# Layer 1's output factor taken from the gated rows' norms, and margins on TensorE's inputs in a list schedule

## The chip, the cores and the metric

One core of one Trainium2 chip runs the whole program. The metric is device time in microseconds (us) of one launch; lower is better. The engines are TensorE (PE, with its weight loads PEld), VectorE (DVE), ScalarE (ACT), GpSimd (POOL) and the queue of SyncE (SP), which issues every DMA.

## What is computed

A top-32 attention over 4 batches of 8 heads, 576 positions of width 64, and behind it two gated layers on the 2304 rows of width 512, each with an inner width of 1536:

```python
scores = q @ k.T / sqrt(64)
kth = np.partition(scores, -32, axis=-1)[..., -32:-31]
attn = softmax(where(scores >= kth, scores, -1e9))
x = (attn @ v) as (2304, 512)
xn = x / sqrt(mean(x * x) + 1e-6) * rms_g
g = xn @ w_gate
x = (g * sigmoid(g) * (xn @ w_val)) @ w_out
out = (sigmoid(x @ w_gate2) * (x @ w_val2)) @ w_out2
```

## The kernel before

Matrix operands are split into two float16 parts, a high and a low one; a product is the sum of three (high by high, high by low, low by high). A part pair needs a scale, a power of two got from a norm, so that its values lie well in float16.

**The work.** The rows come in 18 units of 128. Attention takes a unit in two halves of four tiles. A tile is a head by 128 rows: the score matmuls into `sp` (two buffers of PSUM), VectorE's rounds of maximum and replacement (`m8`, `w`), ScalarE's exponential `e`, the mask on VectorE, the split on ScalarE and POOL into `ph`, a DMA transpose into `pt`, and the product with V into `pv` (`attend`, L687). `enter1` (L801) normalizes a finished unit's rows, splits them into `sn` and has a DMA transpose them into `xt`. `gate1` (L884) does this and, for three pieces j of the inner width, calls `gated` (L839): a product into `pg` and one into `pw`, 48 matmuls each, the tanh and copies by ScalarE, products by POOL into `sg`, and the split into `ht`. `out1` (L892) multiplies the three pieces back into `py` with 144 matmuls and splits it into `yt`. `gate2` and `out2` do the same for layer 2, whose weights `wl` are read again from DRAM for each batch of two units; `out2` adds into `po`.

**The factor.** The scale for the split of `py` comes from `py` itself: ScalarE squares it with a sum per row (`ysq`; the squares go to a scrap tile `junk` under the tag `sn`, the buffer that also holds `enter1`'s input of the transpose), TensorE sums over the partitions with a matrix of ones (`yn`), VectorE makes a power of two of it, and only then ScalarE scales `py` into `sf`:

```python
nc.scalar.activation(junk, py, AF.Square, accum_out=ysq)
t = ps_m.tile([P, 1], F32, name="yn", tag="mm", lane="yn")
nc.tensor.matmul(t, lhsT=ones32, rhs=ysq, start=True, stop=True)
...
s, i = pow2_scale(m, 1, "y")
nc.scalar.activation(f, py, AF.Copy, scale=s)
```

**Buffers.** `pg`, `pw`, `py`, `po`, `yn`, the norms `kvt` and the products of the weight preparation share three banks of PSUM (tag `mm`). The float32 temporaries `wf`, `g`, `sv`, `sf` share four buffers of SBUF (tag `tmp`); `sg` has two, the output tile `acc` two, attention's `xr` one.

**The order.** Nothing is issued as it is written. `Scheduler.record` (L171) notes every operation with its inputs, a cost in ns and a priority that comes from its place in the program, and `order` (L234) plays them forward on a clock of its own: it always takes the operation that can start first, among those of one engine by priority. An operation can start when its inputs are there (L336), its engine is free and a buffer is free for the tile that it opens. Each engine then executes its list strictly in that order. The weights of both layers are converted and scaled in the first part (`prep1`, `prep2`, L541 and L554), beside the first units' attention.

Of the kernel before, what the change touches and what calls it, by code (L numbers as in the profile page):

```python
# [18 lines left out]
P = 128  # L19
# [26 lines left out]
OWN = 130.0  # L46

# [10 lines left out]
BATCHES = (1,) + (2,) * 8 + (1,)  # L58
# [77 lines left out]
class Scheduler:  # L136
# [97 lines left out]
    def order(self):  # L234
# [60 lines left out]
        while len(out) < len(self.ops):  # L295
# [39 lines left out]
            for u in op.users:  # L335
                u.start = max(u.start, op.end + OWN if u.eng == op.eng != "sync" else done)  # L336
# [20 lines left out]
def topk_attention_moe_kernel(  # L357
# [108 lines left out]
    def prep_piece(w, kind, j, g, s, i, place, held, ways):  # L466
# [305 lines left out]
    def attention_rest(b, kv, sc, x):  # L772
# [19 lines left out]
        xr = xp.tile([P, 4, D], F32, name="xr", bufs=1)  # L792
# [8 lines left out]
    def enter1(x):  # L801

        xf = x.rearrange("p h d -> p (h d)")
# [8 lines left out]
        f = m1.tile([P, 512], F32, name="sf", tag="tmp", bufs=4, lane="sfxt")  # L812
# [3 lines left out]
        t = mo.tile([P, 2 * NC, P], F16, name="xt", bufs=1)  # L816
        nc.sync.dma_start_transpose(out=t, in_=n.rearrange("p a d -> p (a d)"))
        return t

    def product(ps, w, xt, start=True, stop=True):  # L820

        with E.group():
            for m in range(4):
                n = 0
                for c in range(4):
                    for l, r in ((c, 0), (c, 1), (c + 4, 0)):
                        nc.tensor.matmul(
                            ps[:, m],
                            lhsT=w[c][:, 512 * r + P * m : 512 * r + P * m + P],
                            rhs=xt[:, l],  # L830
                            start=n == 0,
                            stop=n == 11,
                        )
                        n += 1

    def flat(t):
        return t.rearrange("p m r -> p (m r)")

    def gated(xt, wg, wv, gsc, vsc, silu, name, bufs, last=False, behind=None):  # L839
# [3 lines left out]
        pg = ps_m.tile([P, 4, P], F32, name="pg", tag="mm", lane=name)  # L843
        if behind is not None:
            E.after(behind)
        product(pg, wg, xt)
# [3 lines left out]
        ht = htp.tile([P, 2, CPJ, P], F16, name=name, bufs=bufs)  # L850
        hi, lo = (ht[:, a].rearrange("p m r -> p (m r)") for a in range(2))
        pw = lambda: ps_m.tile([P, 4, P], F32, name="pw", tag="mm", lane=name)
        if last:
            pw = pw()
            product(pw, wv, xt)
# [3 lines left out]
            return ht.rearrange("p a m r -> p (a m) r")  # L859
        if silu:  # L860
            g = m1.tile([P, 512], F32, name="g", tag="tmp", bufs=4, lane="g" + name)
            nc.scalar.activation(g, pg, AF.Copy, scale=gsc)
# [4 lines left out]
        product(pw, wv, xt)  # L867
        sv = m1.tile([P, 512], F32, name="sv", tag="tmp", bufs=4, lane="sv" + name)
# [5 lines left out]
        return ht.rearrange("p a m r -> p (a m) r")  # L874
# [9 lines left out]
    def gate1(u, j):  # L884
        if j == 0:
            in1[u] = enter1(xs[u])
        gsc, vsc, _ = state["c1"]
        ht1[u, j] = gated(
            in1[u], lay1["g"][0][j], lay1["v"][0][j], gsc[:, j : j + 1], vsc[:, j : j + 1], True, "ht1", 3, behind=vsc if u < 2 else None
        )  # L890

    def out1(u):  # L892

        ik = state["c1"][2]
        py = ps_m.tile([P, 4, P], F32, name="py", tag="mm", lane="y")
        with E.group():
            for m in range(4):
                n = 0
                for j in range(NJ):
                    for c in range(4):  # L900
                        for l, r in ((c, 0), (c, 1), (c + 4, 0)):
                            nc.tensor.matmul(
                                py[:, m],
                                lhsT=lay1["o"][0][j][c][:, 512 * r + P * m : 512 * r + P * m + P],
                                rhs=ht1[u, j][:, l],
                                start=n == 0,
                                stop=n == 12 * NJ - 1,
                            )
                            n += 1
        py = flat(py)  # L910
# [7 lines left out]
        s, i = pow2_scale(m, 1, "y")  # L918
        f = m1.tile([P, 512], F32, name="sf", tag="tmp", bufs=4, lane="sfyt")
        nc.scalar.activation(f, py, AF.Copy, scale=s)  # L920
        yt = mo.tile([P, 2, 512], F16, name="yt", bufs=2)
        nc.scalar.activation(yt[:, 0], f, AF.Copy)
        nc.gpsimd.tensor_tensor(out=yt[:, 1], in0=f, in1=yt[:, 0], op=ALU.subtract)
# [4 lines left out]
        in2[u] = (yt.rearrange("p a (c r) -> p (a c) r", r=P), gsc, a)  # L928
# [10 lines left out]
    def gate2(b, u, j):  # L939
        for n in "gv":  # L940
            if (b, n, j) not in w2:
                load2(b, n, j)
        yt, gsc, _ = in2[u]
        last = b == len(batches) - 1
        ht2[u, j] = gated(
            yt, w2[b, "g", j], w2[b, "v", j], gsc[:, j : j + 1], state["c2"][0][:, j : j + 1], False, "ht2", 6, last,
            state["c2"][0] if b == 0 else None
        )

    def out2(b, us):  # L950

        po = {}
        for j in range(NJ):
            load2(b, "o", j)
            for u in us:
                if j == 0:
                    po[u] = ps_m.tile([P, 512], F32, name="po", tag="mm", lane="o")
                w, n = w2[b, "o", j], 0
                with E.group():
                    for c in range(4):  # L960
                        for l, r in ((c, 0), (c, 1), (c + 4, 0)):
                            nc.tensor.matmul(
                                po[u],
                                lhsT=ht2[u, j][:, l],
                                rhs=w[c][:, 512 * r : 512 * r + 512],
                                start=j == 0 and n == 0,
                                stop=j == NJ - 1 and n == 11,
                            )
                            n += 1
        for u in us:  # L970
            osc = tmul(in2[u][2], state["c2"][1], name="osc")
            o = mo.tile([P, 512], F32, name="acc")
            nc.scalar.activation(o, po[u], AF.Copy, scale=osc)
            for dst, rows in dests[u]:
                nc.sync.dma_start(dst, o[rows])


    xs, dests, in1, in2, ht1, ht2, w2, acc, state = {}, {}, {}, {}, {}, {}, {}, {}, {}
    E.prio = -2 * TAU
    gr = m1.tile([P, 512], F32, name="gr", tag="tmp", bufs=4, lane="gr")  # L980
# [48 lines left out]
    batches = [[next(units) for _ in range(n)] for n in BATCHES]  # L1029
    first = lambda us: [(8.1 if j == NJ else 5.4, *((out1, (u,)) if j == NJ else (gate1, (u, j)))) for u in us for j in range(NJ + 1)]  # L1030
    second = lambda b, us: [(5.4, gate2, (b, u, j)) for j in range(NJ) for u in us] + [(7.8 * len(us), out2, (b, us))]
# [3 lines left out]
    for b in range(len(batches) + 1):  # L1035
        lists = [second(b - 1, batches[b - 1]) if b else [], first(batches[b]) if b < len(batches) else []]
# [37 lines left out]
```

## Time and profile before

| | |
|---|---|
| runs | 1255.1, 1255.52, 1259.76 us; median 1255.52 |
| profiled execution | span 1257.2 us, 41569 instructions; the page gives no time of this execution beside its span |
| TensorE busy, by 40 equal slices | `3776474599999999999999999998999999999998` |
| VectorE busy | `6999998897988989888988899787799888970001` |
| granted TensorE clock | `9788576799999999999999999998999999999999` |

The slices are 31.4 us wide and give the busy share in tenths, 9 for 90% or more; the clock is in tenths of full speed. Matmuls are pipelined and their ends are modelled, so the distance from start to start tells more than a duration. A wait is put down to whatever came last.

### The profile page before, as it was taken

To read this page: it belongs to the slowest core of one execution; us is meant where nothing else is said; L and a number is where in the kernel's file an instruction comes from. 1 tells how busy PE (TensorE), PEld (TensorE's weight loads), DVE (VectorE), ACT (ScalarE), POOL (GpSimd) and SP (SyncE) were. 2 spreads that over 40 slices of the span, in tenths; PEclk is the share of its full clock that TensorE was granted. 3 is DMA by queue.
4 is the path that set the end of the run, shared out by engine and by line. 5 is a ranking of instruction groups with operands and counts; after the bars stand their busy time and mean duration, and the time that the engine had idled before them with its cause. 6 is when DMAs were issued, how large, how long until landed. Compare 5 with 4: busy or idle time off the path is not lost.

```text
span 1257.2 us, 41569 instructions
## 1 busy us (share of the span) xinstructions
PE 1128.0 (90%) x17020; PEld 967.0 (77%) x17020; DVE 1006.8 (80%) x2553; ACT 835.8 (66%) x1464; POOL 844.2 (67%) x966
## 2 busy tenths in 40 slices
PE   3776474599999999999999999998999999999998
PEld 2443364598789879969986998798879969997976
DVE  6999998897988989888988899787799888970001
ACT  6999888776596747677854766575847655662531
POOL 6997899887586847685864668475847665761530
PEclk9788576799999999999999999998999999999999
DMA  8986898698977575688978486768685775754337
GB/s 266 289 300 178 232 253 234 177 280 205 203 179 148 131 179 128 146 187 185 225 123 193 110 150 136 180 130 175 139 178 128 152 181 111 183 124 134 136 110 269
DMA packets 323774, 225.26 MB, mean 179 GB/s; under 512 B 278400, under 2 KB 286592, under 8 KB 323584
## 3 DMA queue, kind: packets, MB, share of 16 engines
q1 hardware_dynamic: 323584, 222.62, 72.7%
q8 instruction: 133, 2.18, 0.7%
q14 instruction: 57, 0.47, 0.1%
HBM read 147.06 MB, written 14.16 MB: 128 GB/s over the span
## 4 chain that ended last, share of the span: by engine, by line
PE 45%; DVE 13%; ACT 11%; DMA 10%; POOL 10%; issue 7%; SPq 2%; POOLq 0%; ACTq 0%; DVEq 0%
PE pw L353 13%; PE pg L353 12%; PE po L353 7%; PE py L353 6%; DVE m L353 5%; DVE w L353 4%; DMA pt<-ph 4%; POOL ph L353 3%; POOL sg L353 3%; PE sp L353 3%; PE pv L353 3%; DMA xt<-sn 2%; SPq L353 2%; DMA qt<-qn 2%; POOL ht L353 2%
## 5 line engine op out<-in xcount | busy, mean ns | idle before, releaser
L353 DVE MAX8 m<-w 128x8 f32<-128x576 f32 x432 | 318.1, 751 | 4.3
L353 PEld LDWEIGHTS <-wl 128*128 128x128 f16 x5184 | 294.4, 98 | 3.5 <-issue 1.9
L353 POOL TENSOR_TENSOR ph<-e,ph 128x512 f16<-128x512 f32 (+1 forms) x288 | 204.8, 733 | 86.5 <-ACT ph L353 83.6
L353 DVE MATCH_REPLACE8 w<-m,w 128x576 f32<-128x576 f32 x288 | 213.5, 743 | 0.0
L353 POOL TENSOR_TENSOR sg<-sg,sv 128x512 f32<-128x512 f32 x105 | 133.7, 1274 | 50.2 <-ACT sv L353 47.0
L353 ACT ACTIVATE e<-sp,nb,sc 128x576 f32<-128x576 f32 x144 | 117.3, 829 | 73.1 <-POOL nb L353 37.7
L353 PEld LDWEIGHTS <-w1v 128*128 128x128 f16 (+1 forms) x2640 | 150.2, 98 | 12.3 <-issue 7.5
L353 PE MATMUL pg<-xt,w1g 128*128 128x128 f16 x2592 | 155.7, 221 | 2.9 <-ACT sv L353 1.9
L353 PE MATMUL pg<-yt,wl 128*128 128x128 f16 x2592 | 156.0, 221 | 1.7 <-ACT sv L353 0.8
L353 PE MATMUL pw<-xt,w1v 128*128 128x128 f16 x2592 | 153.5, 219 | 3.6 <-ACT sv L353 3.0
L353 PEld LDWEIGHTS <-w1g 128*128 128x128 f16 (+1 forms) x2624 | 151.4, 99 | 3.7 <-issue 2.3
L353 PE MATMUL pw<-yt,wl 128*128 128x128 f16 x2592 | 153.6, 219 | 0.6 <-ACT sg L353 0.3
L353 POOL TENSOR_TENSOR ht<-sg,ht 128x512 f16<-128x512 f32 x105 | 121.8, 1161 | 45.7 <-ACT ht L353 43.6
L353 PEld LDWEIGHTS <-w1o 128*128 128x128 f16 (+1 forms) x2640 | 150.2, 99 | 1.8 <-DVE w1g L353 1.4
L353 PE MATMUL py<-ht,w1o 128*128 128x128 f16 x2592 | 148.9, 220 | 0.0
L353 PE MATMUL po<-wl,ht 128*128 128x512 f16 x648 | 145.1, 379 | 0.0
L353 PE MATMUL sp<-kt,qt 128*128 128x512 f16 (+3 forms) x640 | 97.8, 300 | 44.7 <-DVE e L353 36.3
L353 ACT ACTIVATE ph<-e 128x576 f16<-128x576 f32 x144 | 97.2, 677 | 53.0 <-DVE e L353 47.1
L353 DVE MAX8 m<-sp 128x8 f32<-128x576 f32 x144 | 108.0, 758 | 28.8 <-PE sp L353 27.9
L353 DVE SCALAR_TENSOR_TENSOR e<-sp,m,e 128x576 f32<-128x576 f32 x144 | 115.6, 810 | 6.2 <-ACT e L353 2.9
L353 PEld LDWEIGHTS <-qt 128*128 128x128 f16 (+1 forms) x640 | 51.3, 104 | 88.8 <-DVE e L353 29.4
L353 PEld LDWEIGHTS <-ht 128*128 128x128 f16 x648 | 61.4, 98 | 69.0
(167 smaller groups left out, 1824.8 us busy)
## 6 DMA issues: line engine op xcount, KB each, us to landing
wl<-w2g SPq DMA_DIRECT2D x60, 512.0 KB, 5.1
wl<-w2v SPq DMA_DIRECT2D x60, 512.0 KB, 4.9
wl<-w2o SPq DMA_DIRECT2D x60, 512.0 KB, 5.0
raw<-in_moe_w_gate_dram SPq DMA_DIRECT2D x24, 512.0 KB, 5.0
raw<-in_moe_w_val_dram SPq DMA_DIRECT2D x24, 512.0 KB, 5.1
raw<-in_moe_w_out_dram SPq DMA_DIRECT2D x24, 512.0 KB, 4.8
qr<-in_q_dram SPq DMA_DIRECT2D x32, 128.0 KB, 2.9
kr<-in_k_dram SPq DMA_DIRECT2D x16, 256.0 KB, 4.5
```

The lines of the kernel that those rows point to most:

```text
L353: getattr(eng, method)(*map(real, a), **{n: real(x) for n, x in k.items()})
```

## The change

Three things change; the other new code (units in groups, halves of a group) is not used here, since every group in `BATCHES` is a single unit, for which the products and their order inside a group are those of before.

- `out1` takes the factor of its split from the gated rows. `gated` squares `sg` in place behind its split, with a sum per row into a column of `hsq` (54 Squares); `out1` adds the three columns on VectorE (`hn`), and `yn` sums that. The factor is the norm's with 2^32 for a bound of the weights, and is there whether `py` is or not. The Square of `py` and its scrap tile go.
- In `order`, past 250000 ns of the planner's own clock, an input of a matmul counts as there 1000 ns later if an engine made it, 2500 ns later if a DMA brought it. Only the order changes; no wait is added. Buffers that come free get no such margin.
- `tmp` has three buffers instead of four; `sg` has three instead of two, which `xr` and `acc` now share.

```diff
+SLACK = (1000.0, 2500.0, 250000.0)
...
             for u in op.users:
-                u.start = max(u.start, op.end + OWN if u.eng == op.eng != "sync" else done)
+                late = SLACK[op.eng == "sync"] if u.eng == "tensor" and op.end > SLACK[2] else 0.0
+                u.start = max(u.start, op.end + OWN if u.eng == op.eng != "sync" else done + late)
...
-                t = m1.tile([P, 512], F32, name="wf", tag="tmp", bufs=4, lane="wf")
+                t = m1.tile([P, 512], F32, name="wf", tag="tmp", bufs=3, lane="wf")
...
-        xr = xp.tile([P, 4, D], F32, name="xr", bufs=1)
+        xr = mo.tile([P, 512], F32, name="xr", tag="sg", bufs=3, lane="xr")[:, 0 : 4 * D].rearrange("p (h d) -> p h d", d=D)
...
-        sg = mo.tile([P, 512], F32, name="sg", lane=name)
+        sg = mo.tile([P, 512], F32, name="sg", bufs=3, lane=name)
...
         nc.scalar.activation(hi, sg, AF.Copy)
         nc.gpsimd.tensor_tensor(out=lo, in0=sg, in1=hi, op=ALU.subtract)
+        if sq is not None:
+            nc.scalar.activation(sg, sg, AF.Square, accum_out=sq)
...
-        ysq = tiny.tile([P, 1], F32, name="ysq")
-        junk = m1.tile([P, 1024], BF16, name="junk", tag="sn", lane="yt")[:, 0:512]
-        nc.scalar.activation(junk, py, AF.Square, accum_out=ysq)
-        t = ps_m.tile([P, 1], F32, name="yn", tag="mm", lane="yn")
-        nc.tensor.matmul(t, lhsT=ones32, rhs=ysq, start=True, stop=True)
-        m = tiny.tile([P, 1], F32, name="ym")
-        nc.vector.tensor_scalar(m, t, 2.0 ** -30, None, op0=ALU.max)
+            n = tiny.tile([P, 1], F32, name="hn")
+            nc.vector.tensor_reduce(n, hsq[b], axis=mybir.AxisListType.X, op=ALU.add)
+            t = ps_m.tile([P, 1], F32, name="yn", tag="mm", lane="yn")
+            nc.tensor.matmul(t, lhsT=ones32, rhs=n, start=True, stop=True)
+            m = tiny.tile([P, 1], F32, name="ym")
+            nc.vector.tensor_scalar(m, t, 2.0 ** -60, 2.0 ** 32, op0=ALU.max, op1=ALU.mult)
...
-            o = mo.tile([P, 512], F32, name="acc")
+                o = mo.tile([P, 512], F32, name="acc", tag="sg", bufs=3, lane="acc")
```

In the orders below a number behind a name is that of a buffer; `wl` is a weight of layer 2, `w1v` and `w1o` are weights of layer 1.

**First place.** TensorE, at the norm of the unit whose `yn` starts at 868.02 us in the trace of before. Before:

```order
L353 MATMUL sp_17721<-kt_17320,qt_17416 64x64
L353 MATMUL kvt_17738<-kvn_17714,ones_0_107 128x1
L353 MATMUL yn_17744<-ysq_17730,ones_0_107 128x1
L353 LDWEIGHTS wl_3164_16889
L353 MATMUL pg_17756<-yt_15208,wl_3164_16889 128x128
```

In the change:

```order
L355 LDWEIGHTS wl_3142_16877
L355 MATMUL pw_17412<-yt_16370,wl_3142_16877 128x128
L355 MATMUL yn_17482<-hn_17332,ones_0_107 128x1
L355 LDWEIGHTS w1o_19_211
L355 MATMUL py_17484<-ht_3109_16560,w1o_19_211 128x128
```

Before, `yn` came after `py` and some attention work; now it comes right ahead of the first matmul of `py`, and reads `hn`.

**Second place.** TensorE, at the last tile of a half of attention, whose `pv` starts at 636.76 us in the trace of before. Before, with the end of the tile ahead of it:

```order
L353 LDWEIGHTS pt_12430
L353 MATMUL pv_12229<-vt_10828,pt_12430 128x65
L353 MATMUL yn_12564<-ysq_12466,ones_0_107 128x1
L353 LDWEIGHTS pt_12477
L353 MATMUL pv_12229<-vt_10828,pt_12477 128x65
```

In the change:

```order
L355 LDWEIGHTS w1v_18_182
L355 MATMUL pw_12725<-xt_12438,w1v_18_182 128x128
L355 LDWEIGHTS pt_12632
L355 MATMUL pv_12456<-vt_11097,pt_12632 128x65
L355 LDWEIGHTS pt_12632
L355 MATMUL pv_12456<-vt_11097,pt_12632 128x64
```

The last tile followed on the third one and a `yn`; now three more groups of 48, `pw`, `pg` and `pw`, have moved in between the scores of that tile and this place, the last of them right ahead.

**Third place.** ScalarE, at the Square, in the same unit as the first place. Before:

```order
L353 ACTIVATE ks_17713,kvn_17714<-kr_17329 128x576
L353 ACTIVATE junk_17731,ysq_17730<-py_17433 128x512
L353 ACTIVATE qr_17147<-qr_17147,qs_17625 128x256
L353 ACTIVATE e_17747<-sp_17703,nb_17742,sc_16997 128x576
L353 ACTIVATE vt_17700<-vr_16268,kvs_16232 128x10x64
```

In the change:

```order
L355 ACTIVATE kr_17329<-kr_17329,kvs_16270 128x576
L355 ACTIVATE sg_17130,hsq_3106_16636<-sg_17130 128x512
L355 ACTIVATE sg_17266<-sg_17266 128x512
L355 ACTIVATE sv_17330<-pw_17217,c_2438_3713 128x512
L355 ACTIVATE junk_17386,ssq_17387<-x_16640 128x512
```

The Square no longer reads `py` from PSUM; it squares `sg` of the unit's last gate, and behind it in the queue stands `sv`, which empties a bank for the next gate.

## Rows read from the trace of the kernel before

**Rows 1.** The page's part 1: busy us, share of the span, instructions.

```profile
PE 1128.0 (90%) x17020; PEld 967.0 (77%) x17020; DVE 1006.8 (80%) x2553; ACT 835.8 (66%) x1464; POOL 844.2 (67%) x966
```

**Rows 2.** Table by stretch: us; PE, PEld, DVE, ACT, POOL busy; clock; DMA; GB/s.

```profile
0.00:250.00 250.00, 150.38 (x1282) 100.54 (x1283) 224.38 (x601) 215.27 (x385) 216.30 (x240) 0.77 0.84 242
250.00:1135.00 885.00, 860.21 (x14131) 769.21 (x14128) 774.25 (x1925) 582.15 (x1019) 597.56 (x701) 1.00 0.74 164
```

**Rows 3.** TensorE's waits, whole span: us in total, times, longest us.

```profile
PE sp L353 <- DVE e L353: 36.3, 8, 8.4
```

**Rows 4.** Timeline of TensorE after attention: start us, us, instruction, shape, count.

```profile
1167.23 2.84 PE L353 MATMUL pg<-yt,wl 128*128 128x128 f16 x48
1169.91 2.84 PE L353 MATMUL pw<-yt,wl 128*128 128x128 f16 x48
```

**Rows 5.** TensorE's waits from 250 us to the end.

```profile
PE pv L353 <- DMA pt<-ph: 8.3, 10, 1.5
PE yn L353 <- ACT junk L353: 6.0, 5, 3.3
PE pg L353 <- ACT sv L353: 2.7, 2, 1.9
PE kvt L353 <- ACT ks L353: 2.1, 2, 1.4
PE sp L353 <- DMA qt<-qn: 1.4, 1, 1.4
PE pg L353 <- DMA xt<-sn: 0.9, 1, 0.9
```

**Rows 6.** Timeline of TensorE at 868 us, [idle before <-releaser].

```profile
868.02 0.58 PE L353 MATMUL yn<-ysq,ones 128*128 128x1 f32 x2 [3.30 <-ACT junk L353]
868.86 5.14 PE L353 MATMUL pg<-yt,wl 128*128 128x128 f16 x48 [0.25 <-DVE kvs L353]
```

**Rows 7.** Table by stretch, from 866.9 to 873.7 us.

```profile
866.90:873.70 6.80, 5.43 (x48) 5.37 (x49) 4.27 (x22) 5.14 (x9) 3.59 (x3) 0.50 0.39 88
```

**Rows 8.** Timeline of ScalarE at 867 us.

```profile
867.28 0.60 ACT L353 ACTIVATE junk<-py 128x512 bf16<-128x512 f32 x1 [3.26 <-DMA xt<-sn]
...
867.87 0.50 ACT L353 ACTIVATE qr<-qr,qs 128x256 f32<-128x256 f32 x1
```

**Rows 9.** Groups by form: busy us, mean ns | idle before.

```profile
L353 POOL TENSOR_TENSOR sg<-sg,sv 128x512 f32<-128x512 f32 x105 | 133.7, 1274 | 50.2 <-ACT sv L353 47.0
L353 POOL TENSOR_TENSOR ht<-sg,ht 128x512 f16<-128x512 f32 x105 | 121.8, 1161 | 45.7 <-ACT ht L353 43.6
...
L353 ACT ACTIVATE ht<-sg 128x512 f16<-128x512 f32 x105 | 65.8, 627 | 73.1 <-POOL sg L353 72.8
...
L353 ACT ACTIVATE sv<-pw,c 128x512 f32<-128x512 f32 x51 | 34.6, 678 | 12.4 <-PE pw L353 12.2
...
L353 ACT ACTIVATE junk<-py 128x512 bf16<-128x512 f32 x18 | 10.6, 589 | 23.6 <-PE py L353 14.0 <-DMA xt<-sn 9.6
...
L353 ACT ACTIVATE junk<-x 128x512 bf16<-128x512 f32 x16 | 10.0, 625 | 9.3 <-DVE x L353 9.3
```

**Rows 10.** Timeline of TensorE at 637 us.

```profile
636.76 0.60 PE L353 MATMUL pv<-vt,pt 128*128 128x65 f16 x14 [1.48 <-DMA pt<-ph]
```

**Rows 11.** The tile `pt`: its transposing DMA, from issue to landing.

```profile
DMA to landing us min/median/max: 3.2/4.1/10.8
```

**Rows 12.** Timeline of TensorE at 537 us.

```profile
537.42 2.84 PE L353 MATMUL pg<-xt,w1g 128*128 128x128 f16 x48 [1.91 <-ACT sv L353]
```

**Rows 13.** Timeline of TensorE in the opening.

```profile
238.01 1.14 PE L353 MATMUL sp<-kt,qt 128*128 128x512 f16 x4 [7.69 <-DVE e L353]
...
248.29 3.22 PE L353 MATMUL pg<-xt,w1g 128*128 128x128 f16 x48
```

**Rows 14.** Groups by form, VectorE and ScalarE.

```profile
L353 DVE MAX8 m<-w 128x8 f32<-128x576 f32 x432 | 318.1, 751 | 4.3
...
L353 ACT ACTIVATE wf<-wh,ws 128x512 f32<-128x512 f32 x36 | 24.4, 719 | 0.8 <-DVE ws L353 0.8
```

More of the change, by code (lines that the diff above doesn't have):

```diff
@@ L815, in enter1 @@
         nc.gpsimd.tensor_tensor(out=n[:, 1], in0=f, in1=n[:, 0], op=ALU.subtract)
[L816 to L820, printed above, removed]
-        with E.group():
[L823 to L834, printed above, removed]
+        nc.sync.dma_start_transpose(out=in1[b][:, i], in_=n.rearrange("p a d -> p (a d)"))
@@ new lines, in spread, with columns, product @@
+    def spread(b):
+        return CPJ // len(groups[b]), len(groups[b])
+    def columns(b, tiles):
+        M = spread(b)[0]
+        return lambda c, a: tiles[c // M][:, a, c % M]
+    def product(ps, b, k, ws, rhss):
+        M = spread(b)[0]
+        with E.group():
+            for m in range(M):
+                o = P * (k * M + m)
+                n, last = 0, 12 * len(ws) - 1
+                for w, rhs in zip(ws, rhss):
+                    for c in range(CPJ):
+                        for a, r in ((0, 0), (0, 1), (1, 0)):
+                            nc.tensor.matmul(
+                                ps[:, m],
+                                lhsT=w[c][:, 512 * r + o : 512 * r + o + P],
+                                rhs=rhs(c, a),
+                                start=n == 0,
+                                stop=n == last,
+                            )
+                            n += 1
@@ L853, in gated @@
+        hi, lo = (flat(ht[:, a]) for a in range(2))
+        pw = lambda: ps_m.tile([P, M, U, P], F32, name="pw", tag="mm", lane=name)
         if last:
             pw = pw()
-            product(pw, wv, xt)
+            product(pw, b, k, [wv], [rhs])
             nc.vector.scalar_tensor_tensor(out=sg, in0=sg, scalar=1.0, in1=flat(pw), op0=ALU.add, op1=ALU.mult)
@@ L866, in gated @@
         pw = pw()
-        product(pw, wv, xt)
-        sv = m1.tile([P, 512], F32, name="sv", tag="tmp", bufs=4, lane="sv" + name)
+        product(pw, b, k, [wv], [rhs])
+        sv = m1.tile([P, 512], F32, name="sv", tag="tmp", bufs=3, lane="sv" + name)
         E.after(sg)
@@ L890, in gate1, with out1 @@
         )
-    def out1(u):
+    def out1(b, k):
         ik = state["c1"][2]
[L895 to L910, printed above, removed]
-        ysq = tiny.tile([P, 1], F32, name="ysq")
-        junk = m1.tile([P, 1024], BF16, name="junk", tag="sn", lane="yt")[:, 0:512]
-        nc.scalar.activation(junk, py, AF.Square, accum_out=ysq)
-        t = ps_m.tile([P, 1], F32, name="yn", tag="mm", lane="yn")
-        nc.tensor.matmul(t, lhsT=ones32, rhs=ysq, start=True, stop=True)
-        m = tiny.tile([P, 1], F32, name="ym")
-        nc.vector.tensor_scalar(m, t, 2.0 ** -30, None, op0=ALU.max)
[L918 to L923, printed above, removed]
@@ new lines, in out1 @@
+        s, i = ys[b]
+        py = ps_m.tile([P, M, U, P], F32, name="py", tag="mm", lane="y")
+        product(
+            py, b, k, [lay1["o"][0][j] for j in range(NJ)],
+            [columns(b, [ht1[b, j, x] for x in range(U)]) for j in range(NJ)],
+        )
+        f = m1.tile([P, 512], F32, name="sf", tag="tmp", bufs=3, lane="sfyt")
+        nc.scalar.activation(f, flat(py), AF.Copy, scale=s)
+        yt = mo.tile([P, 2, M, U, P], F16, name="yt", bufs=2)
+        hi, lo = (flat(yt[:, a]) for a in range(2))
@@ L948, in gate2, with out2 @@
         )
-    def out2(b, us):
+    def out2(d):
         po = {}
         for j in range(NJ):
[L954 to L971, printed above, removed]
-            o = mo.tile([P, 512], F32, name="acc")
-            nc.scalar.activation(o, po[u], AF.Copy, scale=osc)
-            for dst, rows in dests[u]:
-                nc.sync.dma_start(dst, o[rows])
@@ L978, in topk_attention_moe_kernel @@
-    xs, dests, in1, in2, ht1, ht2, w2, acc, state = {}, {}, {}, {}, {}, {}, {}, {}, {}
+            load2(d, "o", j)
+            w = w2[d, "o", j]
+            for b in batches[d]:
+                ht = columns(b, [ht2[b, j, k] for k in range(len(groups[b]))])
+                for x, u in enumerate(groups[b]):
+                    if j == 0:
+                        po[u] = ps_m.tile([P, 512], F32, name="po", tag="mm", lane="o")
+                    n = 0
+                    with E.group():
+                        for c in range(4):
+                            for a, r in ((0, 0), (0, 1), (1, 0)):
+                                nc.tensor.matmul(
+                                    po[u],
+                                    lhsT=ht(c, a)[:, x],
+                                    rhs=w[c][:, 512 * r : 512 * r + 512],
+                                    start=j == 0 and n == 0,
+                                    stop=j == NJ - 1 and n == 11,
+                                )
+                                n += 1
@@ L979, in topk_attention_moe_kernel @@
+        for b in batches[d]:
+            for u in groups[b]:
+                osc = tmul(in2[b][2], state["c2"][1], name="osc")
+                o = mo.tile([P, 512], F32, name="acc", tag="sg", bufs=3, lane="acc")
+                nc.scalar.activation(o, po[u], AF.Copy, scale=osc)
+                for dst, rows in dests[u]:
+                    nc.sync.dma_start(dst, o[rows])
+    xs, dests, in1, in2, ht1, ht2, w2, hsq, ys, yts, state = {}, {}, {}, {}, {}, {}, {}, {}, {}, {}, {}
     E.prio = -2 * TAU
-    gr = m1.tile([P, 512], F32, name="gr", tag="tmp", bufs=4, lane="gr")
+    gr = m1.tile([P, 512], F32, name="gr", tag="tmp", bufs=3, lane="gr")
@@ L1028, in topk_attention_moe_kernel @@
     units = iter(range(len(dests)))
[L1029 to L1031 removed]
+    groups, batches = [], []
+    for batch in BATCHES:
+        batches.append([])
+        for n in batch:
+            batches[-1].append(len(groups))
+            groups.append([next(units) for _ in range(n)])
+    halves = lambda b: range(len(groups[b]))
+    first = lambda d: [
+        i for b in batches[d]
+        for i in [(5.4, gate1, (b, j, k)) for j in range(NJ) for k in halves(b)] + [(8.1, out1, (b, k)) for k in halves(b)]
+    ]
+    second = lambda d: [(5.4, gate2, (d, b, j, k)) for j in range(NJ) for b in batches[d] for k in halves(b)] + [
+        (7.8 * sum(len(groups[b]) for b in batches[d]), out2, (d,))
+    ]
     pos = 0.0
```

75 lines of the change are left out of this document (46 added, 29 removed).

## The prediction

> **What bounds the kernel now.** I read the page's busy line first, then a table by stage, then TensorE's waits, then the instructions around the longest ones. [Rows 1]: TensorE is busy 90% of the span of 1257.2 us, more than any other engine. [Rows 2] split that by stage. Up to 250 us TensorE works 150.4 of 250 us, at a granted clock of 0.77, while VectorE is busy 224.4 us: there the other engines set the pace, and the longest wait is the scores for VectorE's masking [rows 3]. From 250 to 1135 us TensorE is busy 860.2 of 885 us, and from there to the end it has matmuls alone. So past the opening the time is TensorE's work plus its gaps. The work has no slack of its own: with the clock at 1.00, groups of 48 matmuls start 2.68 us apart [rows 4], 55.8 ns a matmul, and the change neither adds nor removes such a matmul. What can be won or lost is the gaps.
>
> [Rows 5] list who ended them. Two kinds lead: the second attention product `pv` for the transposed probabilities, 8.3 us in 10 waits, none over 1.5, and the norm matmul `yn` for ScalarE's Square, 6.0 us in 5, the longest 3.3. [Rows 6] show that longest one: `yn` starts 3.30 us late, and the 48 matmuls behind it take 5.14 us where [rows 4] show 2.84; the granted clock of that stretch is 0.50, its lower level of 1.2 GHz [rows 7]. [Rows 8] say why: ScalarE came to the Square late because its scrap output shares a buffer (tag `sn`) with the input of the transpose `xt`, and waited 3.26 us for that DMA.
>
> **The change, part by part.** *The factor from the gated rows.* The Square of `py`, 18 times, goes, and with it the wait of `yn` for it. In the order for the unit of [rows 6], `yn` no longer stands behind two score tiles and a `kvt` after `py`; it stands right before `py`, as in 14 of 18 units. Its inputs are Squares of `sg`, issued gate by gate. Between the last value product of a unit and its `yn` the new order has 12.6 us of matmul work or more, 8.0 in the last unit (counted at the start-to-start times of this trace); what has to be done in it is one evacuation of 0.68, a POOL product of 1.27, a cast of 0.63, a POOL subtraction of 1.16 and the Square, some 4.4 us [rows 9]. I take all 6.0 us as gone, and the 2.3 us (5.14 less 2.84) of low clock behind the longest: **-8.3**.
>
> What it adds is 54 Squares on ScalarE, in place. On this engine a Square and its accumulator read hold the queue 0.59 us ([rows 8]: 867.28 to 867.87); from SBUF instead of PSUM the Square is 0.04 longer, 625 against 589 ns [rows 9]. That is 54 x 0.63 - 18 x 0.59 = 23.4 us more work on an engine that idles 303 of the 885 us [rows 2]: nothing on the path as long as no bank of PSUM waits behind it. But each Square overwrites `sg`, so it waits for POOL's subtraction that still reads it, and behind it in the queue stand evacuations and exponentials. The 18 added reductions on VectorE are of three elements and lie beside TensorE.
>
> *The margins.* Past 250 us of the planner's clock, a matmul counts as ready 1.0 us after an engine's result is there and 2.5 us after a DMA's. No wait is added; groups move. In the second excerpt the product that waited 1.48 us [rows 10] has moved behind three more groups: between its scores and it stand 240 matmuls of groups before (`pw`, `py`, `pg`) and 384 now, 13.4 against 21.4 us at 55.8 ns. Over tiles 24 to 143 the mean of that lead, in matmul work, rises from 20.5 to 23.0 us and its least value from 15.6 to 17.6. All ten waits of `pv` are shorter than the 2.5 us gained: **-8.3** (at worst half, where transposes land late: 4.1 us is the median and 10.8 the longest [rows 11]). The query transpose (1.4) and `xt` (0.9) go likewise, **-2.3**, and of the norms of K (2.1, the longest 1.4, against a margin of 1.0) I take **-1.5**.
>
> What stays: 2.7 us of `pg` for ScalarE's `sv` [rows 5]. These are waits for a bank of PSUM to come free, and the margins are put on inputs alone. [Rows 12] show the worst: `pg` waited 1.91 us for the bank that the gate product before it, two small `kvt` back, had just filled. In the new order that place stands with still less work between (0.5 against 0.9 us), and of 277 turn-overs of the three banks 22 now have under 3 us, 11 before. I add as much again: **+2.7**. And `xt` has 16.1 us from the last `pv` to the first gate in two late units, under any of the late ones before: **+1.0**.
>
> *The opening.* The margins do not apply there, but the smaller rings (`tmp` three buffers for four, `sg` three shared with `xr` and `acc`) change the order from about 115 us. VectorE's masking of tiles 18 and 20 stands behind 7.6 and 2.0 us less work, and the first gate of the second unit is now ahead of the scores of tile 23 and of the last weight piece; before, it started at 248.29, right after scores that had waited for VectorE, some of them 7.69 us [rows 13]. Against that, the last four scale reductions of layer 2's weights stand behind 5.8 to 10.4 us more (eleven maxima and replacements of about 0.75 us, and smaller ones [rows 14]), and one of them blocks TensorE. I take **-2**, between -10 (all stalls of the second unit gone) and +10.4.
>
> **The sum.** -8.3 - 8.3 - 2.3 - 1.5 + 2.7 + 1.0 - 2 = -18.7. The page gives a span of 1257.2 and no time beside it; the median of the three runs, 1255.5, is 1.7 lower. 1257.2 - 18.7 = 1238.5, and 1.7 less is **1237 us**, 1.5% faster. With the bounds of `pv` (+4.2) and of the opening (-8, +12.4): 1229 to 1253.
>
> **The rivals.** *The opening wins too:* the second unit's gates fill the stalls that [rows 3, 13] show, -10 for -2: **1229**. For it, xt's chain there has up to 11.8 us less ScalarE work in front; against, VectorE paces those microseconds and its sum is unchanged.
>
> *Only the norm wait goes:* margins move a wait rather than end it, as the in-order queue stops at the next late input. Then only 8.3 is won: **1247**. The mean lead of 2.5 us speaks against it; that DMA landings scatter over 7.6 us [rows 11] for it.
>
> *The opening pays:* the late weight pieces and the smaller `tmp` ring lengthen it by 10.4: 1237 + 2 + 10.4 = **1249**, about no change. The ring's place is the layer-2 pieces: 36 times ScalarE writes `wf` and POOL reads it in a subtraction of the 1.16 us of [rows 9]; with four buffers ScalarE idles 0.8 us before them in all [rows 14], and POOL, 216 of 250 us busy [rows 2], may be late by one more. The Trainium skill (Perfetto Trace Analysis, Optimization Strategy) says that consistent bubbles can mean too little SBUF or PSUM for the next tile, which speaks against shrinking a ring; no run here shows it yet.
>
> *Slower:* the Squares hold back evacuations. Place: ScalarE's queue, behind POOL's subtraction. If each of the 54 holds a bank that TensorE wants for its 0.63 us, that is 34 us on top: **1271**. It decides from 0.46 us each on (25 us: the 18.7 won and 6.3 more). Against it: only 22 of 277 turn-overs are tight; ScalarE has a third of its time free.
>
> **Chances.** A measurement of this kernel can tell about 0.5% (6.3 us) from no change. Forecast 0.54, opening wins 0.10, norm wait alone 0.14, opening pays 0.14, Squares 0.08. Faster: the first two, most of the third (0.10) and a little of the fourth (0.04), 0.78. Same 0.14, slower 0.08. The range leaves out the Squares and the tails: 1226 to 1253.
>
> **What would show it.** After 250 us: no wait of `yn` for ScalarE, `pv` under 2 us in all, granted clock 1.00 throughout, and TensorE's waits from the 21.4 us that [rows 5] list to about 8, led by banks (`pg` or `pw` for `sv`). First gate of the second unit at 240 to 248 us. Wrong, if `pv` still waits over 4 us, if banks wait over 10, or if gates start after 255.

## The result, and the profile after

The change runs in 1244.80 us (median of four runs, 1243.03 to 1248.31) against 1257.64 us for the kernel before, measured again beside it (four runs, 1255.10 to 1260.55). The ratio is 0.9894, 95% interval 0.9868 to 0.9921: 12.8 us or 1.1% faster. The profiled execution of the change has a span of 1246.5 us and took 1248.31 us; it is the slowest of the four.

The page's busy line and the table by stretch of the change answer to [rows 1] and [rows 2], in the same columns:

```profile
PE 1128.9 (91%) x17020; PEld 966.5 (78%) x17020; DVE 999.0 (80%) x2571; ACT 859.3 (69%) x1536; POOL 844.8 (68%) x966
```

```profile
0.00:250.00 250.00, 156.57 (x1351) 104.86 (x1352) 223.55 (x596) 215.75 (x390) 216.13 (x239) 0.80 0.83 241
250.00:1135.00 885.00, 865.13 (x14106) 769.02 (x14105) 768.14 (x1951) 606.37 (x1088) 600.78 (x704) 0.99 0.75 166
```

ScalarE is busy 23.5 us more in all, which is the 23.4 that the Squares were costed at. But from 250 us to 1135 TensorE idles 19.9 us where it idled 24.8, five less. That is far under the gain that was looked for, until the stretch is cut finer. First before, then the change (columns as in [rows 2]):

```profile
250.00:350.00 100.00, 95.54 (x1627) 86.79 (x1624) 90.64 (x240) 67.64 (x123) 68.66 (x80) 1.00 0.90 220
350.00:600.00 250.00, 244.15 (x3989) 217.32 (x3987) 224.84 (x564) 175.66 (x310) 175.59 (x204) 1.00 0.75 162
600.00:850.00 250.00, 242.86 (x3962) 216.34 (x3959) 218.60 (x538) 159.97 (x280) 167.48 (x199) 1.00 0.74 157
850.00:1135.00 285.00, 277.66 (x4567) 248.76 (x4564) 240.18 (x586) 178.88 (x309) 185.83 (x220) 0.99 0.68 151
```

```profile
250.00:350.00 100.00, 88.96 (x1419) 78.57 (x1418) 87.17 (x237) 68.76 (x125) 69.03 (x82) 0.95 0.93 220
350.00:600.00 250.00, 245.46 (x4038) 218.83 (x4033) 218.27 (x562) 176.27 (x318) 168.75 (x197) 1.00 0.75 161
600.00:850.00 250.00, 247.48 (x4066) 221.78 (x4063) 225.72 (x562) 172.40 (x312) 174.28 (x205) 1.00 0.72 158
850.00:1135.00 285.00, 283.23 (x4600) 249.83 (x4598) 236.98 (x592) 188.94 (x334) 188.71 (x223) 1.00 0.70 157
```

From 350 to 1135 us TensorE's idle time falls from 20.3 to 8.8 us: this is where the change works. From 250 to 350 us it rises from 4.5 to 11.0, and 208 fewer matmuls run there: here the change pays. Ahead of 250 us it is in front, with 1351 matmuls run for 1282.

A tally from the matmul records puts both in one measure, and takes in the low clock that idle time misses. The *gap* of a matmul is the time to the next one's start, less what its columns take at the full clock (55.8 ns for 128, as in [rows 4]; a record of a float32 matmul counts twice that). Summed, before had 142.4 us of gaps to 350 us and 31.5 behind; the change has 149.6 and 13.5. So 18.0 us are won past 350 us, and 7.2 lost ahead of it. The loss lies between 250 and 350 us: there the gaps rise from about 5.5 to 16.1 us, while ahead of 250 us they fall from about 137 to 133.5.

TensorE's waits of the change from 250 us to the end answer to [rows 5] (us in total, times, longest us):

```profile
PE sp L355 <- DVE e L355: 5.8, 4, 3.2
PE pg L355 <- ACT g L355: 3.2, 3, 1.5
PE pv L355 <- DMA pt<-ph: 2.5, 2, 1.9
PE po L355 <- ACT g L355: 1.7, 1, 1.7
PE kvt L355 <- ACT ks L355: 1.2, 1, 1.2
...
PE pg L355 <- ACT sv L355: 0.4, 1, 0.4
```

The line of `yn` is gone and the ten waits of `pv` have become two, both ahead of 350 us. Two kinds are new: `pg` and `po` for ScalarE's `g`, the second read of a gate's bank. The wait of the scores for VectorE's `e` has grown from 0.9 us (one wait, in the same list of before) to 5.8, of which 4.2 lie ahead of 350 us. The last `yn` of the change, in the unit with the shortest lead, now starts on time and `py` right behind it (timeline of TensorE, no bracket, so no wait; the view ends inside `py`):

```profile
1194.34 2.75 PE L355 MATMUL po<-wl,ht 128*128 128x512 f16 x12
1196.93 0.28 PE L355 MATMUL yn<-hn,ones 128*128 128x1 f32 x2
1197.07 3.12 PE L355 MATMUL py<-ht,w1o 128*128 128x128 f16 x53
```

What was lost ahead of 350 us shows in the same view at 260 us, before and then the change:

```profile
260.23 0.65 PE L353 MATMUL sp<-kt,qt 128*128 128x512 f16 x4
260.72 2.84 PE L353 MATMUL pg<-xt,w1g 128*128 128x128 f16 x48
263.40 2.84 PE L353 MATMUL pg<-yt,wl 128*128 128x128 f16 x48
266.08 0.65 PE L353 MATMUL sp<-kt,qt 128*128 128x512 f16 x4
```

```profile
241.30 4.81 PE L355 MATMUL pg<-xt,w1g 128*128 128x128 f16 x48
...
266.60 0.56 PE L355 MATMUL kvt<-kvn,ones 128*128 128x1 f32 x4
270.34 1.12 PE L355 MATMUL sp<-kt,qt 128*128 128x512 f16 x4 [3.18 <-DVE e L355]
271.93 1.12 PE L355 MATMUL sp<-kt,qt 128*128 128x512 f16 x4 [0.47 <-DVE qs L355]
272.86 0.96 PE L355 MATMUL pv<-vt,pt 128*128 128x65 f16 x14
273.63 9.40 PE L355 MATMUL py<-ht,w1o 128*128 128x128 f16 x144
282.87 1.34 PE L355 MATMUL pg<-yt,wl 128*128 128x128 f16 x21
```

Before, gates of layer 2 (`pg<-yt`) ran between the scores from 263.40 us on. In the change the first of them comes at 282.87 (the view ends inside it), and the scores wait 3.18 us for VectorE with nothing to fill the time. Behind that wait the clock is at its lower level (table by stretch):

```profile
269.30:276.20 6.90, 5.39 (x47) 4.17 (x47) 6.90 (x20) 4.84 (x9) 6.15 (x7) 0.51 1.00 377
```

So the low stretch of [rows 7] is gone, and another has come, behind another wait of about the same length.

Layer 2 begins late together with its weights. The last of their scales (`w2oi`, on VectorE) comes 8.4 us later than before, and SyncE's first loads of the finished weights (`wl`) 11.6 us later (timelines of VectorE and of SyncE, before and then the change):

```profile
248.79 0.14 DVE L353 TENSOR_SCALAR w2oi<-ws 128x1 int32<-128x1 int32 x1
255.93 1.25 SPq L353 DMA_DIRECT2D wl<-w2g  x2
```

```profile
257.23 0.14 DVE L355 TENSOR_SCALAR w2oi<-ws 128x1 int32<-128x1 int32 x1
267.49 1.36 SPq L355 DMA_DIRECT2D wl<-w2g  x2
```

### The profile page after: what moved, and what is told of

Its sections match the earlier page's. It is cut to its first block, busy times and chain, and to the rows that moved or that the text cites. A ratio compares the mean times of both kernels' runs of the same rounds, so it can differ in the third digit from the quotient of the medians.

```text
span 1246.5 us, 41715 instructions
## 1 busy us (share of the span) xinstructions
PE 1128.9 (91%) x17020; PEld 966.5 (78%) x17020; DVE 999.0 (80%) x2571; ACT 859.3 (69%) x1536; POOL 844.8 (68%) x966
## 4 chain that ended last, share of the span: by engine, by line
PE 55%; DVE 14%; ACT 13%; issue 6%; POOL 6%; DMA 5%; SPq 2%; ACTq 0%; DVEq 0%; POOLq 0%
PE pg L355 14%; PE pw L355 14%; PE po L355 10%; PE py L355 8%; DVE m L355 5%; DVE w L355 5%; PE sp L355 3%; PE pv L355 3%; POOL ph L355 2%; SPq L355 2%; ACT raw L355 1%; ACT e L355 1%; ACT sg L355 1%; POOL sg L355 1%; DVE e L355 1%
## 5 line engine op out<-in xcount | busy, mean ns | idle before, releaser
L355 ACT ACTIVATE ht<-sg 128x512 f16<-128x512 f32 x105 | 65.8, 627 | 70.1 <-POOL sg L355 69.7
```

What stands on the lines that cost most here:

```text
L355: getattr(eng, method)(*map(real, a), **{n: real(x) for n, x in k.items()})
```

## The experiments

All twelve in one table: the median time, its ratio to the kernel before on the same chip with the 95% interval, the gaps of the profiled execution to 350 us and past it, and the start of the first gate of layer 2 in us. "Edits" says what differs from the change.

| kernel | edits | us | ratio | to 350 | past 350 | layer 2 |
|---|---|---|---|---|---|---|
| before | | 1257.6 | | 142.4 | 31.5 | 263.4 |
| the change | | 1244.8 | 0.9894 (0.9868 to 0.9921) | 149.6 | 13.5 | 282.9 |
| e1 | no margins | 1259.2 | 1.0005 (0.9977 to 1.0032) | 146.9 | 26.1 | 279.2 |
| e2 | before + margins | 1257.7 | 0.9987 (0.9966 to 1.0009) | 144.5 | 28.5 | 264.4 |
| e3 | old rings | 1251.8 | 0.9936 (0.9914 to 0.9957) | 147.5 | 18.6 | 271.5 |
| e4 | margins from 350 us | 1248.7 | 0.9903 (0.9866 to 0.9940) | 148.3 | 15.2 | 282.3 |
| e5 | factor from 5th unit | 1243.6 | 0.9869 (0.9841 to 0.9897) | 145.8 | 10.9 | 269.3 |
| e6 | margin on banks too | 1248.2 | 0.9902 (0.9873 to 0.9930) | 145.7 | 18.6 | 281.7 |
| e7 | DMA margin only | 1245.8 | 0.9887 (0.9856 to 0.9918) | 145.8 | 15.1 | 280.8 |
| e8 | margins doubled | 1259.2 | 0.9997 (0.9976 to 1.0019) | 151.6 | 23.6 | 281.2 |
| e9 | before + DMA margin | 1253.9 | 0.9956 (0.9932 to 0.9980) | 144.1 | 28.4 | 264.3 |
| e10 | each Square twice | 1258.0 | 0.9977 (0.9957 to 0.9998) | 146.2 | 24.6 | 268.1 |
| e11 | margins halved | 1249.2 | 0.9908 (0.9881 to 0.9935) | 150.0 | 21.4 | 283.6 |
| e12 | e5 and e7 together | 1251.4 | 0.9915 (0.9892 to 0.9938) | 148.0 | 18.6 | 271.4 |

Gaps are of one execution each. The profiled ones of the change, e9 and e11 lie 3.5, 3.8 and 7.9 us above their medians, so their gaps are on the high side. How far two executions of one order lie apart e5 and e12 show: TensorE's order is the same in both up to 328 us, and their gaps to 350 us are 145.8 and 148.0.

### The two parts apart: e1, e2, e9

e1 is the change without its margins, e2 the kernel before with the margins alone (its `order` as in the change's diff, with the same `SLACK`).

```diff
-SLACK = (1000.0, 2500.0, 250000.0)
+SLACK = (0.0, 0.0, 250000.0)
```

> The change with both margins at 0: the factor from the gated rows and the smaller rings stay. Theory A (factor and margins each remove their own waits past 350 us, and what was lost between 250 and 350 us comes from the rings' new order of the opening): no wait of yn for ScalarE, but pv for pt again 5 to 8 us past 350 us, excess between 250 and 350 us still over 10, time 1249 to 1253. Theory B (the loss between 250 and 350 us comes from margins that set in while VectorE still sets the pace): that stretch back near before's 5 us, time 1240 to 1246. Theory C (the margins do it all): 1255 to 1260.

> The kernel before with the margins alone (1000 and 2500 ns past 250000 ns), Square of py and old rings kept. Theory A: pv under 3 us past 250 us, yn still 4 to 8 us, no loss between 250 and 350 us, time 1244 to 1250. Theory B: a loss of some 10 us between 250 and 350 us, time 1250 to 1256. Theory C: 1243 to 1246.

Neither moves the time: both intervals hold 1. That is later than Theory A gave for each of them. The time of e1 is that of Theory C (the margins do it all), which e2 refutes, and e2 lies above all three of its ranges. Together the same two parts give 1.1%. By the gaps past 350 us the factor alone (with the new rings) is worth 5.4 us, the margins alone 3.0, both 18.0, so 9.6 us come only where they meet. Ahead of 350 us e1 loses 4.5 and e2 2.1 of that again. The waits from 250 us say what each lacks. First e1:

```profile
PE pv L355 <- DMA pt<-ph: 14.2, 12, 2.5
```

then e2:

```profile
PE pw L355 <- DVE ym L355: 5.1, 9, 1.1
PE pg L355 <- DVE ym L355: 3.5, 3, 2.7
PE pv L355 <- DMA pt<-ph: 2.7, 2, 1.4
```

With the factor alone the wait of `yn` for a Square goes, but `pv` waits 14.2 us where it waited 8.3 [rows 5]. The increase lies between 250 and 350 us (6.7 for 1.3); past 350 us `pv` waits 7.6 us for 7.0, so there the factor leaves it as it was. With the margins alone `pv` falls to 2.7, but gates and values wait 8.6 us for `ym`. `ym` reads the small bank of `yn`, and it is also the first step from `yn` to the scale with which `py` is evacuated; the margin on `yn`'s input from ScalarE puts that chain later.

e9 tests this: the old factor with the DMA's margin alone, so that `yn` gets none.

```diff
-SLACK = (1000.0, 2500.0, 250000.0)
+SLACK = (0.0, 2500.0, 250000.0)
```

> The kernel before with the margin of 2.5 us on a DMA's result alone; py's Square and the order of yn as before. Theory A (beside the old factor both margins gained nothing because the engines' margin puts yn another 1.0 us behind py's Square, and so holds py's bank for the chain of Square, yn, ym and evacuation; the DMA margin alone has no such price): pg's and pw's waits for ym fall from 8.6 us to under 4 past 250 us, pv's under 4, yn's for the Square 3 to 7, time 1249 to 1254 us. Rival (with the old factor the banks are held too long for any margin): pg and pw wait 7 us or more for ym, time 1256 to 1261 us.

The waits from 250 us of e9:

```profile
PE yn L355 <- ACT junk L355: 3.6, 3, 1.6
...
PE pw L355 <- DVE ym L355: 0.9, 3, 0.4
...
PE pg L355 <- DVE ym L355: 0.6, 2, 0.4
PE pv L355 <- DMA pt<-ph: 0.5, 1, 0.5
```

The waits for `ym` fall from 8.6 to 1.5 us, those of `yn` for the Square are 3.6, and the time is 0.4% under before (0.9932 to 0.9980), inside what Theory A gave. So the engines' margin did bring the waits for `ym`. That their end makes the kernel faster than e2 is not shown: the two intervals overlap, and the gaps past 350 us are 28.4 and 28.5 us, other waits having come.

### Which margin, and how wide: e7, e11, e8

All three change one line of the change: `SLACK` begins with 0 and 2500 ns in e7, 500 and 1250 in e11, 2000 and 5000 in e8.

> The change with the margin of 2.5 us on a DMA's result alone, none on an engine's. Theory A (beside the new factor it is pv's wait for the transposes that takes the gain back, so the DMA margin is the whole of the margins' worth): pv waits under 4 us past 250 us, time 1243 to 1247 us. Rival (the engines' margin does its half, for kvt, pw and yn): waits of pw, kvt and yn for engines rise to 6 us or more, time 1249 to 1254 us.

> The change with margins of 0.5 and 1.25 us, half of its own. Theory A (what the margins win grows with the part of pv's waits that they cover, the longest of which are 2.5 us without them): pv waits 4 to 7 us past 250 us, time 1248 to 1253 us. Rival (half is enough, most waits are under 1.25 us): pv under 4 us, time 1243 to 1247 us. Another rival (the times with margins are one order's luck each): any time from 1243 to 1260 us, with no order between none, half, whole and double in pv's waits.

> The change with margins of 2.0 and 5.0 us for 1.0 and 2.5. Theory A (the margins of the change already cover the scatter, pv waits 2.5 us in all; more of it buys nothing and holds results longer): time 1243 to 1248 us, pv under 2 us, waits for banks as before or 2 to 4 us more. Rival (the scatter is wider than 2.5 us and part of what is left comes from it): time 1237 to 1241 us.

e7 runs as fast as the change (1245.8 us), with 1.5 us of `pv` waits and 4.7 of `kvt`. Beside the new factor the margin on engines' results adds nothing that these runs show.

In width the medians are 1259.2 us without margins, 1249.2 at half, 1244.8 at the change's and 1259.2 at twice that. The waits of `pv` from 250 us on go with them: 14.2, 8.7, 2.5 and 7.3 us. The time at half is what Theory A gave, its 8.7 us of waits are over the 4 to 7. Half and the whole cannot be told apart by time (their intervals overlap almost wholly), and each width is one order, so no more of a curve is shown than that either is better than none and than twice. That twice the margin loses everything neither theory had. The waits of e8 from 250 us:

```profile
PE sp L355 <- DVE e L355: 10.9, 7, 2.8
PE pv L355 <- DMA pt<-ph: 7.3, 3, 3.7
PE yn L355 <- ACT acc L355: 1.7, 2, 1.0
```

Scores wait for VectorE 10.9 us, nearly twice the 5.8 of the change, and `pv` is back at 7.3. A margin is paid in the order: every matmul held back delays what reads its result, and VectorE, busy 764 and 768 of the 885 us in the two kernels, has little room to catch up. That is my reading of the rows; no run holds VectorE's part alone. From 350 to 1120 us VectorE itself waits 18.5 us for TensorE's `kvt` in e8, and 3.8 in the change; but in e1, with no margins, it waits 11.6.

### The banks: e6

e6 gives PSUM's buffers a margin too: in the planner they count as free 1000 ns after their last reader.

```diff
-                    r["free"].append(t.end)
+                    r["free"].append(t.end + (BANK if t.pool.space == PSUM and op.end > SLACK[2] else 0.0))
```

> The change, and past 250 us of the planner's clock a bank of PSUM counts as free only 1.0 us after its reader is done. Theory A (what is left past 250 us are waits for banks: pg, po and pw for ScalarE's g, py for acc, some 7 us): those waits fall to under 2 us in all, time 1237 to 1241 us. Rival (the margin moves groups back to where inputs are late, or the scores behind VectorE take the place): pv or sp waits rise by as much, time 1243 to 1248 us.

```profile
PE sp L356 <- DVE e L356: 5.9, 5, 3.3
PE pv L356 <- DMA pt<-ph: 5.2, 4, 1.9
PE yn L356 <- ACT acc L356: 2.1, 1, 2.1
```

These are the longest waits from 250 us. `pg`, `po` and `pw` for `g`, 5.7 us in the change, are gone altogether, and the time is not better: `pv` waits 2.7 us more and `yn` 2.1 for a bank that it did not wait for. Theory A falls, and the rival is nearer, with 1248.2 us just over its range. Bank waits were real, but with these gone by the order others came in their place.

### The opening: e3, e4, e5

e3 puts the old rings back (`tmp` four buffers, `sg` two, `xr` and `acc` with their own), e4 starts the margins at 350000 ns instead of 250000, and e5 lets the first four units take their factor from `py`'s Square as before (`LATE = 4`):

```diff
-            behind=vsc if groups[b][0] < 2 else None, sq=hsq[b][:, j * U + k : j * U + k + 1],
+            behind=vsc if groups[b][0] < 2 else None,
+            sq=hsq[b][:, j * U + k : j * U + k + 1] if b >= LATE else None,
...
+        if b < LATE:
+            ysq = tiny.tile([P, 1], F32, name="ysq")
...
+            nc.scalar.activation(junk, flat(py), AF.Square, accum_out=ysq)
```

> The change with the rings of before (tmp four buffers, sg two, xr and acc on their own). Theory A: TensorE's waits between 250 and 350 us fall from 16 us towards 5, the rest as in the change, time 1233 to 1240. Theory B: that stretch stays at 12 us or more, time 1242 to 1248.

> The change with the margins from 350000 ns of the planner's clock on instead of 250000. Theory A: the stretch from 250 to 350 us keeps 12 us or more, time 1242 to 1248. Theory B: it comes back to 5 to 8 us and the waits past 350 us stay away, time 1233 to 1240.

> The change, but the first four units of layer 1 take their factor from py's Square as before; the gated rows' factor starts with the fifth unit. Theory A (the 12 Squares of the first four units crowd ScalarE while it still scales the weights, and so cost the 7 us by which the change is behind the kernel before at 350 us): TensorE's gaps up to 350 us fall from 149.6 us to 142 to 145, those past 350 us stay at 13 to 15, time 1238 to 1241 us. Rival (the loss is only how the list schedule falls out, whatever is computed): gaps to 350 us stay at 147 to 151, time 1244 to 1250 us.

e4 is the change again (148.3 and 15.2 us of gaps), so no cost of the margins' early start shows. In the traces TensorE's order is that of the change up to 272 us in e1, e4, e7 and e8 alike, so the late start of layer 2 was settled without the margins. e3 has only 6.9 us of gaps from 250 to 350 us, where the change has 16.1, but 140.6 ahead of 250 for 133.5: the smaller rings move the loss, and the sum to 350 us is nearly the same, 147.5. The time of e3 is above both expectations and 0.4% above the change's by the ratios, and the intervals just overlap. The old rings as a whole are not better than the new here; `tmp` by itself no run changes.

e5 brings the first gate of layer 2 from 282.9 to 269.3 us and the gaps to 350 us from 149.6 to 145.8, just over the 142 to 145 that Theory A gave. Its time of 1243.6 us is above the 1238 to 1241 expected, and its interval overlaps the change's. That falls between the two theories, and e12, with e5's order up to 328 us, does not repeat the 145.8.

### The Squares' cover: e10

```diff
             nc.scalar.activation(sg, sg, AF.Square, accum_out=sq)
+            nc.scalar.activation(sg, sg, AF.Square, accum_out=tiny.tile([P, 1], F32, name="sq2"))
```

> The change with each of the 54 Squares of the gated rows issued twice, the second into an accumulator that nobody reads: 54 more instructions of some 0.63 us on ScalarE, 34 us. Theory A (past 250 us ScalarE has room for the Squares; only those of the first units, some 12 in the opening, cost): gaps past 350 us stay at 13 to 16 us, those to 350 us rise by 2 to 6 us, time 1245 to 1251 us. Rival (Squares hold back evacuations, as the slower case of the forecast has it): waits of TensorE for ScalarE past 350 us rise by 8 us or more, time above 1253 us.

1258.0 us: the doubled Squares take back nearly all of the gain, and past 350 us the gaps are 24.6 us for 13.5. By time and size the rival is nearer, but not by its path: TensorE's waits for ScalarE past 350 us are 4.6 us, where the change has 6.3. What grew is the wait of scores for VectorE, from 250 us on:

```profile
PE sp L355 <- DVE e L355: 12.9, 11, 3.5
```

One of these can be followed. On VectorE, then on TensorE:

```profile
390.03 0.16 DVE L355 TENSOR_REDUCE hn<-hsq 128x1 f32<-128x3 f32 x1 [3.94 <-ACT sg L355]
...
391.81 0.82 DVE L355 SCALAR_TENSOR_TENSOR e<-sp,m,e 128x576 f32<-128x576 f32 x1
```

```profile
390.18 0.65 PE L355 MATMUL sp<-kt,qt 128*128 128x512 f16 x4
392.68 0.66 PE L355 MATMUL sp<-kt,qt 128*128 128x512 f16 x4 [1.85 <-DVE e L355]
```

The small reduction `hn` stands in VectorE's queue and waits 3.94 us for the Square on ScalarE; the masking `e` behind it is late too, and the next scores wait 1.85 us. In the change itself `hn` waits 0.7, 0.4 and 1.0 us while attention runs, so this path is nearly closed there. It is one wait of the eleven. From 350 to 1120 us VectorE's waits for these Squares grow from 2.1 to 7.8 us, but those for TensorE's `kvt` grow more, from 3.8 to 14.9, so `hn` is shown as one path and not as the whole.

Up to 350 us e10 has 146.2 us of gaps, fewer than the change. That speaks against a cost of the opening's Squares by their time on ScalarE, and so against Theory A of e5. Both kernels have another order in the opening than the change, and in both layer 2 begins sooner. So it does in e3, and in all three VectorE's `w2oi` of the kind shown above comes sooner than in the change: at 250.3 us in e3, 250.4 in e10 and 254.0 in e5, for 257.2. The late weights of layer 2 thus go with its late start over these kernels. That they cost the time is not shown: e3 has them early and has 7.1 us more of gaps than the change ahead of 250 us.

### A version of both: e12

e12 is e5 with the `SLACK` of e7.

> The two edits together that each left the change's time as it was or a little lower: the new factor from the fifth unit on, and the margin of 2.5 us on DMA results alone. Theory A (the first removes some 4 us of the gaps to 350 us, the second loses nothing past it): gaps to 350 us 142 to 147, past it 10 to 14, time 1239 to 1244 us. Rival (each order falls out anew): time 1244 to 1250 us.

1251.4 us, above both expectations: the two edits do not add. Past 350 us its gaps are 18.6 us, with neither parent over 15.1. No kernel of this set is shown to beat the change; e5 alone has the lower median, by 1.2 us. What is shown beyond one order is the gain itself: all eight kernels that have the new factor (in e5 and e12 from the fifth unit on), single Squares and a margin no wider than the change's (the change, e3 to e7, e11 and e12) lie under before, at 0.987 to 0.994. Differences of a few us among them can be the luck of an order.

## Why the prediction was right, and where it was off

The forecast was faster by 1.5%, 1237 us in 1226 to 1253; it is faster by 1.1%, at 1244.8. It misses by 7.8 us, in two parts. **The anchor**, 1.9: the sum was set against the median of three runs, 1255.5, by taking an execution's time as 1.7 us under its span. The change's profiled execution took 1248.31 us with a span of 1246.5, so the time is 1.8 above the span, and the four runs of before have a median of 1257.6. **The gain**, 5.9: 12.8 us for 18.7.

- *Past the opening* the size was right only if the opening ends at 350 us. The forecast was 16.7 us (the sum without the opening); the gaps past 350 us fell by 18.0, and the waits listed there fall from 20.8 to 9.0 us. From 250 us on, where the prediction set its border, the gaps fell by some 7 us, and the waits listed are 19.9 us, not about 8; scores for VectorE lead, not banks.
- *The factor, -8.3:* the waits of `yn` from 250 us on are gone in the change, and in e3, e4, e7 and e10 too, and so is the low stretch of [rows 7].
- *`pv`, -8.3:* 2.5 us are left, against the 2 that were called the limit, and none of it past 350 us.
- *Banks, +2.7 on 2.7,* was too small: `pg`, `pw`, `po` and `py` wait 8.0 us for ScalarE from 250 us on, 6.3 of it past 350. The reader was not `sv`, as [rows 12] led me to think, but `g` for most of it.
- *The adding up* was wrong, though the sum came out. The terms of the factor and of the margins were priced one by one, as if each could be had alone. e1 and e2 show that neither can: 5.4 and 3.0 us, not 8.3 and 12. That the two together gave the sum is luck as far as the prediction goes, which had no term for their meeting. The mechanism of the rival "only the norm wait goes" (the in-order queue stops at the next late input) shows in e1 between 250 and 350 us, where `pv` waits 6.7 us for 1.3.
- *The opening, -2,* is the step that failed. Up to 250 us it came out: the first gate of the second unit came at 241.3 us, in the 240 to 248 named, and the gaps fell by some 3.5 us. But the late weight pieces stood in the term only as a bound, 10.4, set against what the early gate wins, and were not followed to the start of layer 2: from 250 to 350 us the gaps rose by some 10.7, so that to 350 us they grew by 7.2 us in the two profiles. Over the eight kernels with the change's rings and the new factor in every unit (the change, e1, e4, e6, e7, e8, e10, e11) they are 148.0 on average, over the three with the old factor throughout (before, e2, e9) 143.7: +4.3 for -2, which is 6.3 us and about the whole shortfall of the gain. The rival "the opening pays" named the late pieces and the ring. The pieces were late, by 8.4 us for the last scale of layer 2's weights, within the 5.8 to 10.4 named, and the scores that follow one another with no layer-2 work between them, at 270 us, are what the late start of layer 2 looks like. A cost of the rings e3 does not show, and what sets the loss stays open.
- *Clock 1.00 after 250 us* was wrong for the same reason: two low stretches remain, at 269 and 327 us.
- *The Squares at nothing* held in the change: ScalarE's 23.5 us more show in no wait of their own beside the banks. e10 shows how near the limit may be. With 54 further ones the time is some 10 us longer by the ratios, 0.19 us each if it is all theirs, and one path of it is one that the prediction did not have (`hn` in VectorE's queue). The text said of `hn` only that it lies beside TensorE, and did not name what is queued behind it.

The Trainium skill (Perfetto Trace Analysis, Optimization Strategy) was quoted against the smaller ring: consistent bubbles can mean too little room for the next tile. The runs here do not bear it out for the rings as a whole: with the old ones (e3, `tmp` with four buffers and `sg` with two) the gaps past 350 us are 18.6 us, with the new (three and three) 13.5. For `tmp` alone no run here shows it either way.

## What to carry to other kernels

In an in-order queue a wait removed and leads widened need not add up, so price the two together, and test each alone (here each alone moved the time by nothing, both together by 1.1%). A planner's margin can be too wide as well as too narrow, and the width is found by runs (here 2.5 us on DMA results won, and 5.0, with the engines' margin doubled as well, did not). Put it first on the inputs that scatter, the DMA's: that margin alone did all that both did here. On a short chain that holds a bank it brought new waits. Look at a reshuffled opening apart from the rest, and to its end: in the two profiles it lost 7.2 us of the 18.0 that the steady part won, behind a first gate that came early as forecast.

## What the runs showed that I had not expected

- Twice a margin that wins 1% wins nothing (1259.2 us, as with none).
- The time of an execution lies some 2 us above its span (1248.31 for 1246.5; 1242.20 for 1240.1).
- Of two waits of the same kind and nearly the same length one was followed by the lower clock and one not. In the change `py` behind the wait of 3.18 us takes 9.40 us for 144 matmuls; at 853 us, with 1.00 granted, 144 of them take 8.20. In e5 the same kind of wait, 3.12 us long, has groups of 48 at the full 2.84 us right behind it (timeline of TensorE):

```profile
261.51 0.65 PE L356 MATMUL sp<-kt,qt 128*128 128x512 f16 x4 [3.12 <-DVE e L356]
262.00 2.84 PE L356 MATMUL pg<-xt,w1g 128*128 128x128 f16 x48
```

So the prediction's 2.3 us of low clock behind the longest wait was what that one wait cost, not a price of every wait of 3 us. What tells the two apart no run here shows.
